# Linear attention and two expert layers on one core: attention steps of two batches moved by a slot, saved weight combinations paced anew, a result copy and six stores moved

## The chip, the cores and the metric

The kernel runs on one core of a Trainium2 chip. The metric is the device time of one execution in microseconds (us). An executed kernel has five engines with a queue of instructions each: PE (matrix products), DVE and ACT (elementwise work), POOL and SP (here mainly the issuing of DMAs). The engines work side by side and wait for each other by semaphores.

## The reference, cut to what matters

Four batches of eight heads, 576 positions and 64 channels per head. Attention is linear: a softmax over channels for q, one over positions for k, then two small products. Its result is x, 2304 tokens by 512, and passes through two layers:

```
q_s = softmax(q, over channels); k_s = softmax(k, over positions)
x = q_s @ (k_s^T @ v)                       # per batch and head
x = ((x @ w1) * (x @ w2)) @ w3 @ w_out      # 512 -> 1024 -> 512
p = domain_probs / sum(domain_probs)
out = sum over e of p[:, e] * (relu(x @ e1[e]) @ e2[e])   # four experts
```

All inputs are fp32, and every product here is made of three matmuls of a high and a low part (`mm3`, lines 106 to 110; `split`, line 101, makes the two parts: the high one by ACT, line 102, the low one by DVE, line 103).

## The kernel before, in words

The program has three stages. **Stage one** (0 to 272 us in the profile) reads the weights of the first layer, folds `w3 @ w_out` into one matrix `W`, and computes attention batch by batch. **Tokens** go in five chunks of 512, the last of 256 (numbers 0 to 4). For each chunk and each of eight slices `f` of the hidden layer, `ab_step` makes `x @ w1` and `x @ w2`, `h_step` splits their product into `h`, and `y_step` adds `h @ W` into four PSUM banks; `y_out(c)` copies the four banks into `yt` tiles (ACT, line 517) and stores them to DRAM. The `y_step`s of chunks 0 and 1 come in one loop of 16 steps, the Y loop (217 to 272 us), since `W` is ready only then. Chunk 2 follows (to 360 us), then chunks 3 and 4 together (to 455 us).

**Attention** of the later batches is cut into steps that stand in tables by slot and run between the steps of the layer: for each pair of heads `k_max` in slot s (its PE work is `mt`, lines 212 and 216, its ACT copy `mx`, line 220), `k_exp` in s+1, `k_v` in s+2 (PE `kv`, line 245, ACT `bd`, line 257), `x_stage` in s+3 (PE `xp`, line 326, then a split into `x`). The queries go in `q_exp`, `q_norm` and `q_turn` (PE `qt`, line 313). In batches 2 and 3 `mt`, `kv`, `qt` and `xp` share two PSUM banks.

**Combinations.** The third stage multiplies blocks of the experts' weights by a scheme with fewer products, and wants sums of weight blocks, split in two. For many expert blocks these are made ahead ("cooked") and saved to DRAM: `cooking` loads raw weights into two buffers (`e1r`, `e2r`, 1 MB), `cook` lists the parts and sums; a part is a `split` into one of five `eo` tiles (ACT, then DVE), a sum is one DVE instruction (line 586); `save_e` stores an `eo` by an SP DMA (line 606; `e_a<-eo`, `e_s<-eo`, `e_t<-eo`, `e_b<-eo`). `cook_some(k)` takes the next k of these. In the program before it takes two per step of the Y loop from its fourth step, four per step of chunk 2, and eight per step of chunks 3 and 4, and all that are left in step `NF-3`.

**Stage three** (455 to 1168 us) is the expert layer: PE lines 876 and 950, with loads of weights `eg`. At its end `store` (line 836) writes each of 18 tiles of 128 tokens in two halves by SP DMAs; the last six tiles come last.

The program's order is not the order on an engine: a scheduler that estimates times lays out the instructions of every engine, so moving a step in the code moves other rows too. The sections below show such rows. What fixes an order without a wait is `hold(key, inst)`, which makes an instruction stand behind those in `gate[key]`.

Of the kernel before, what the change touches and what calls it, by code (L numbers as in the profile page):

```python
# [8 lines left out]
F32 = mybir.dt.float32  # L9
# [4 lines left out]
ALU = mybir.AluOpType  # L14
# [23 lines left out]
X_SLOT = [AB0, AB1, REST, REST + 8]  # L38
# [16 lines left out]
def linear_attention_moe_kernel(ctx: ExitStack, tc, q, k, v, w1, w2, w3, wo, dp, e1, e2, out):  # L55
    nc = tc.nc
    w1, w2, w3, wo = (w.bitcast(I32) for w in (w1, w2, w3, wo))
    B, H, S, D = q.shape
    NT, DM = out.shape
    NF = w1.shape[1] // 256  # L60
    E = e1.shape[0]
    P = 128
# [6 lines left out]
    QP, QR = 64, 9  # L69
# [15 lines left out]
    def gran(name):  # L85
        return gp.tile([P, 2, 512], F32R, tag="g", name=name)

    def raw(name, pool=gp):
        return pool.tile([P, 1024], F32, tag="g", name=name)
# [10 lines left out]

    def split(hi, lo, src, eng=nc.vector):
        i = nc.scalar.activation(out=hi, in_=src, func=ACTF.Copy)  # L102
        eng.tensor_tensor(out=lo, in0=src, in1=hi.bitcast(F32), op=ALU.subtract)  # L103
        return i

    def mm3(ps, w_hi, w_lo, r_hi, r_lo, first, last, shared=False):
        kw = {"skip_group_check": True} if shared else {}
# [4 lines left out]
    gate = {}  # L112

    def after_inst(inst, other):
        tc.add_manual_dep(inst.ins, other.ins.name, ORDER, reason="order")

    def hold(key, inst):
        for other in gate.get(key, []):
            after_inst(inst, other)
# [231 lines left out]
    before, mid, after = {}, {}, {}  # L351

    def put(d, slot, f, *a):
        d.setdefault(slot, []).append((f, a))

    def run(d, slot):
        for f, a in d.pop(slot, []):
            f(*a)

    for b in range(B):  # L360
        for j in range(2):
            s = Q_SLOT[b][j]
            if b > 0:
                put(before, s - 2, load_q, b, j)
            put(before, s, q_exp, b, j)
            put(before, s + 1, q_norm, b, j)
            for g in range(3):
                put(after, s + 1, q_turn, b, j, g)
        for i, hp in enumerate(PAIRS):
            s = K_SLOT[b][i]  # L370
            if b > 0:
                put(before, s - 3, load_kv, b, hp)
            put(before, s, k_max, b, hp)
            put(before, s + 1, k_exp, b, hp)
            put(mid, s + 2, k_v, b, hp)
            put(after, min(s + 3, X_SLOT[b] - 1), x_stage, b, hp)

# [65 lines left out]
    def load_w12(c, f):  # L445
        for i in range(2):
            g = gran("wg")
            gate["dma"] = [nc.sync.dma_start(out=g.bitcast(F32), in_=w12d[f, i])]
            w12.setdefault((c, f), []).append(g)
        if c == NC - 2:  # L450
            w12[NC - 1, f] = w12[c, f]
# [8 lines left out]
    hg, yps, Wg, prods, ps_z = {}, {}, {}, {}, []  # L460
# [22 lines left out]
    def h_step(c, f):  # L483
        n = chunks[c][1]
        h = gran("h")
        split(h[:, 0, 0:n], h[:, 1, 0:n], prods[c, f // 2][:, f % 2, 0:n])
        if f % 2:
            del prods[c, f // 2]
        hg[c, f] = h
# [22 lines left out]
    def y_out(c):  # L512
        j0, n = chunks[c]
        for dd in range(2):
            t = raw("yt").rearrange("p (k f) -> p k f", k=2)
            for k in range(2):
                nc.scalar.activation(
                    out=t[:, k, 0:n], in_=yps[c, 2 * dd + k], func=ACTF.Copy
                )
            nc.sync.dma_start(out=yd[:, 2 * dd:2 * dd + 2, j0:j0 + n], in_=t[:, :, 0:n])  # L520
# [38 lines left out]
    ewd, ew, tok, yraw = {}, {}, {}, {}  # L559
# [11 lines left out]
    def load_e(kind, n, pool):  # L571
        e, m = n // 2, n % 2
        r = pool.tile([P, 2048], F32, tag="R", name=f"{kind}r")
        for hf in range(2):
            o = 512 * hf + 256 * m
            if kind == "e1":
                dst = r.rearrange("p (h k f) -> p h k f", h=2, k=KT)
                src = e1[e][:, o:o + 256].rearrange("(k p) f -> p k f", p=P)
            else:
                dst = r.rearrange("p (h u f) -> p h u f", h=2, u=2)  # L580
                src = e2[e][o:o + 256, :].rearrange("(u p) f -> p u f", p=P)
            nc.sync.dma_start(out=dst[:, hf], in_=src)
        return dst
# [4 lines left out]
    def cook(kind, n, r, part):  # L588
        q11, q12, q21, q22 = QUARTERS[kind](r)
        if kind == "e1":  # L590
            return [
                part("a11", q11), part("a12", q12), part("a22", q22),
                minus(q22, q21, q22, ALU.add), minus(q21, q11, q21), part("s1", q22),
                minus(q11, q22, q11), part("s3", q21), minus(q12, q12, q11),
                part("s2", q11), part("s4", q12),
            ]
        return [
            part("b11", q11), part("b21", q21), part("b22", q22),
            minus(q11, q12, q11), minus(q12, q22, q12), part("t1", q11),
            minus(q22, q22, q11), part("t3", q12), minus(q21, q21, q22),  # L600
            part("t2", q22), part("t4", q21),
        ]

    def save_e(kind, n, name, g):
        ewd[kind, n, name] = d = dr.tile([P, 2, 2, 256], F32, name=f"{kind}_{n}_{name}")
        nc.sync.dma_start(out=d, in_=g.bitcast(F32))
# [4 lines left out]
    def cooking(pool):  # L611
        raws_e, waiting = {}, []

        def ask(i):
            if i < len(COOKED):
                raws_e[i] = load_e(*COOKED[i], pool)

        def part_of(kind, n):
            def part(name, src):
                def do():  # L620
                    g = pool.tile([P, 2, 2, 256], F32R, tag="o", name="eo", bufs=NOUT)
                    split(g[:, 0], g[:, 1], src)
                    waiting.append((kind, n, name, g))
                return do
            return part

        ask(0)
        yield
        for i, (kind, n) in enumerate(COOKED):
            ask(i + 1)  # L630
            for do in cook(kind, n, raws_e.pop(i), part_of(kind, n)):
                do()
                while len(waiting) > 2:
                    save_e(*waiting.pop(0))
                yield
        while waiting:
            save_e(*waiting.pop(0))
# [32 lines left out]
    def slot(s, *steps):  # L670
        run(before, s)
        for f, *args in steps:
            f(*args)
            run(mid, s)
        run(mid, s)
        run(after, s)
# [69 lines left out]
    kitchen = ExitStack()  # L746
# [3 lines left out]
    def cook_some(k):  # L750
        for _ in range(k):
            next(cooks, None)

    for i, (c, f) in enumerate(steps):
        if c == 1 and f >= NF - 2:
            load_w12(2, f - NF + 2)
        if i + 4 < len(steps):
            h_step(*steps[i + 4])
        slot(Y0 + i, (y_step, c, f))
        if i > 2:  # L760
            cook_some(2)
        if f == NF - 1:
            y_out(c)

# [13 lines left out]
        run(after, REST + f)  # L778
    x_free(2)
    y_step(2, NF - 1)  # L780
    y_out(2)
    att.close()
    two = ExitStack()
    ps_z.append(two.enter_context(tc.tile_pool(name="ps_z", bufs=2, space=PSUM)))
    for f in range(NF):
        if f + 2 < NF:
            load_w12(3, f + 2)
        run(before, REST + NF + f)
        for c in (3, 4):
            ab_step(c, f)  # L790
            h_step(c, f)
            cook_some(4)
        run(mid, REST + NF + f)
        for c in (3, 4):
            if f > 0:
                y_step(c, f - 1)
        run(after, REST + NF + f)
        if f == NF - 3:
            cook_some(200)
            kitchen.close()  # L800
            yp_ = ctx.enter_context(tc.tile_pool(name="yp", bufs=1, side="right"))
            tp = ctx.enter_context(
                tc.tile_pool(name="tok", bufs=7, side="right", reuse_waits="tile")
            )
            ep = ctx.enter_context(
                tc.tile_pool(name="e", bufs=9, side="right", reuse_waits="tile")
            )
            load_y(0)
            first_tok = tset(0)
        if f >= NF - 3:  # L810
            for g in first_tok[4 * (f - NF + 3):4 * (f - NF + 4)]:
                g()
        if f == NF - 2:
            for name in USE["e1"]:
                load_cooked("e1", 0, name)
    for c in (3, 4):
# [12 lines left out]
    acc, blocks, hs = {}, {}, {}  # L829
    NN = 3 * NGE  # L830

    def store(t):
        for hf in range(2):
            b, n = divmod(2 * t + hf, QR)
            dst = out[S * b:S * b + S].rearrange("(q n) d -> n q d", n=QR)
            nc.sync.dma_start(out=dst[n], in_=acc[t][QP * hf:QP * hf + QP])

    def run_some(works, k, of):
        for work in works:
# [222 lines left out]
```

## Time and profile before

| what | us |
|---|---|
| median of three runs | 1174.22 (1173.98 to 1175.68) |
| the profiled execution | 1177.03 |
| its span, first to last instruction | 1175.3 |
| PE busy in it | 1132.6 |
| DVE, ACT, POOL busy | 866.1, 534.8, 49.4 |
| mean granted PE clock | 0.988 of full |

The span is what the rows below measure; the execution's own time is 1.7 us longer. A window row gives the busy time of each engine in a stretch, then the clock granted to PE as a share of its full 2.4 GHz (0.50 is 1.2 GHz), the busy share of the DMA engines and their GB/s. The chain is the work that ended last, followed back from the end. A timeline row gives a start, a duration, and in brackets how long the engine stood before it and what it waited for.

### The profile page before, as it was taken

To read this page: it belongs to the slowest core of one execution; us is meant where nothing else is said; L and a number is where in the kernel's file an instruction comes from. 1 tells how busy PE (TensorE), PEld (TensorE's weight loads), DVE (VectorE), ACT (ScalarE), POOL (GpSimd) and SP (SyncE) were. 2 spreads that over 40 slices of the span, in tenths; PEclk is the share of its full clock that TensorE was granted. 3 is DMA by queue.
4 is the path that set the end of the run, shared out by engine and by line. 5 is a ranking of instruction groups with operands and counts; after the bars stand their busy time and mean duration, and the time that the engine had idled before them with its cause. 6 is when DMAs were issued, how large, how long until landed. Compare 5 with 4: busy or idle time off the path is not lost.

```text
span 1175.3 us, 18720 instructions
## 1 busy us (share of the span) xinstructions
PE 1132.6 (96%) x7048; PEld 1053.3 (90%) x7048; DVE 866.1 (74%) x1428; ACT 534.8 (46%) x982; POOL 49.4 (4%) x70
## 2 busy tenths in 40 slices
PE   5889999989999999999999999999999999999997
PEld 4666888768788889999999999999999999999997
DVE  7898867765557312999989987777779777777776
ACT  4655535554445213655545543444445344444441
POOL 0002300012001000000000000000000000000000
PEclk9889999989999999999999999999999999999999
DMA  9998960699899903877786888777777787777773
GB/s 241 276 349 275 358 224 21 218 370 413 287 369 356 352 29 134 332 287 286 287 286 252 281 309 302 251 253 249 251 251 247 257 300 253 250 252 251 247 254 96
DMA packets 127418, 310.12 MB, mean 264 GB/s; under 512 B 31968, under 2 KB 52960, under 8 KB 127328
## 3 DMA queue, kind: packets, MB, share of 16 engines
q1 hardware_dynamic: 127328, 308.92, 76.6%
q8 instruction: 56, 0.92, 0.3%
q14 instruction: 34, 0.28, 0.1%
HBM read 232.33 MB, written 76.55 MB: 263 GB/s over the span
## 4 chain that ended last, share of the span: by engine, by line
PE 86%; DVE 4%; DMA 4%; ACT 1%; SPq 1%; issue 1%; DVEq 0%; ACTq 0%
PE hp L876 29%; PE op L950 27%; PE ab L108 6%; PE ab L109 6%; PE ab L110 6%; PE y L108 2%; PE y L109 2%; PE y L110 2%; PE kv L245 1%; DVE acc L934 1%; DMA qr<-in_q_dram 1%; DMA eg<-e_b 1%; PE W L108 1%; PE W L109 1%; PE W L110 1%
## 5 line engine op out<-in xcount | busy, mean ns | idle before, releaser
L950 PE MATMUL op<-eg,h 128*128 128x256 f32 x3024 | 379.9, 280 | 0.9 <-DMA eg<-e_b 0.8
L876 PE MATMUL hp<-t,eg 128*128 128x384 f32 x2016 | 376.8, 336 | 0.9 <-DVE acc L934 0.9
L950 PEld LDWEIGHTS op<-eg,h 128*128 128x128 f32 x3024 | 373.4, 188 | 1.4 <-PE hp L876 1.1
L876 PEld LDWEIGHTS hp<-t,eg 128*128 128x128 f32 x2016 | 344.6, 188 | 2.8 <-DVE acc L934 1.9
L934 DVE SCALAR_TENSOR_TENSOR acc<-op,prob,acc 128x256 f32<-128x256 f32 (+1 forms) x396 | 197.2, 527 | 43.2 <-PE op L950 43.1
L102 ACT ACTIVATE h<-blk 128x768 fp32r<-128x768 f32 x168 | 138.0, 842 | 144.1 <-DVE blk L586 109.9
L103 DVE TENSOR_TENSOR h<-blk,h 128x768 fp32r<-128x768 f32 x168 | 157.2, 951 | 24.0 <-ACT h L102 23.9
L859 ACT ACTIVATE blk<-hp 128x384 f32<-128x384 f32 x192 | 90.5, 489 | 140.9 <-PE hp L876 139.1
L863 DVE TENSOR_TENSOR blk<-hp,blk 128x384 f32<-128x384 f32 x144 | 79.4, 556 | 67.3 <-PE hp L876 66.8
L108 PE MATMUL ab<-x,wg 128*128 128x512 f32 (+1 forms) x320 | 122.4, 384 | 4.7 <-ACT wg L102 2.7
L109 PE MATMUL ab<-x,wg 128*128 128x512 f32 (+1 forms) x320 | 120.7, 377 | 0.2 <-ACT x L347 0.2
L110 PE MATMUL ab<-x,wg 128*128 128x512 f32 (+1 forms) x320 | 120.1, 378 | 0.0
L865 ACT ACTIVATE blk<-blk 128x768 f32<-128x768 f32 x72 | 60.6, 845 | 73.7 <-DVE blk L863 72.2
L586 DVE TENSOR_TENSOR blk<-blk 128x768 f32<-128x768 f32 x96 | 91.4, 952 | 0.5
L108 PEld LDWEIGHTS ab<-x,wg 128*128 128x128 f32 x320 | 61.2, 192 | 16.1 <-ACT wg L102 3.2
L109 PEld LDWEIGHTS ab<-x,wg 128*128 128x128 f32 x320 | 61.8, 193 | 10.9 <-ACT x L347 0.8
L480 DVE TENSOR_TENSOR ah<-ab,ah 128x512 f32<-128x512 f32 (+1 forms) x40 | 25.4, 634 | 62.3 <-PE ab L110 56.0
L110 PEld LDWEIGHTS ab<-x,wg 128*128 128x128 f32 x320 | 61.6, 193 | 10.6
L103 DVE TENSOR_TENSOR eo<-e2r,eo 128x512 fp32r<-128x512 f32 x56 | 39.8, 719 | 29.9 <-ACT eo L102 29.9
L109 PE MATMUL y<-h,W 128*128 128x512 f32 x128 | 50.9, 399 | 1.4 <-DVE h L103 1.4
L102 ACT ACTIVATE h<-ah 128x512 fp32r<-128x512 f32 (+1 forms) x40 | 22.8, 589 | 64.0 <-DVE ah L480 64.0
L110 PE MATMUL y<-h,W 128*128 128x512 f32 x128 | 50.2, 398 | 0.0
(98 smaller groups left out, 1068.2 us busy)
## 6 DMA issues: line engine op xcount, KB each, us to landing
eg<-e_t SPq DMA_DIRECT2D x96, 512.0 KB, 4.6
eg<-e_b SPq DMA_DIRECT2D x72, 512.0 KB, 5.2
eg<-e_s SPq DMA_DIRECT2D x68, 512.0 KB, 4.4
eg<-e_a SPq DMA_DIRECT2D x51, 512.0 KB, 4.6
wg<-w SPq DMA_DIRECT2D x48, 512.0 KB, 8.8
f<-in_moe_w_dram SPq DMA_DIRECT2D x32, 512.0 KB, 6.4
e_t<-eo SPq DMA_DIRECT2D x32, 512.0 KB, 6.2
e_s<-eg SPq DMA_DIRECT2D x28, 512.0 KB, 3.9
```

Source lines behind the costliest of these rows:

```text
L102: i = nc.scalar.activation(out=hi, in_=src, func=ACTF.Copy)
L103: eng.tensor_tensor(out=lo, in0=src, in1=hi.bitcast(F32), op=ALU.subtract)
L108: nc.tensor.matmul(out=ps, lhsT=w_hi, rhs=r_hi, start=first, stop=False, **kw)
L109: nc.tensor.matmul(out=ps, lhsT=w_hi, rhs=r_lo, start=False, stop=False, **kw)
L110: nc.tensor.matmul(out=ps, lhsT=w_lo, rhs=r_hi, start=False, stop=last, **kw)
L586: return lambda: nc.vector.tensor_tensor(out=dst, in0=x, in1=y, op=op)
L859: nc.scalar.activation(out=block(name)[:, u], in_=src, func=func)
L863: nc.vector.tensor_tensor(out=x[:, u], in0=src, in1=x[:, u], op=ALU.add)
L865: nc.scalar.activation(out=x, in_=x, func=ACTF.Relu)
L876: nc.tensor.matmul(out=q, lhsT=w[:, sw, kt, P * u:P * u + P], rhs=t[b][:, kt, st], start=new and kt == 0 and i == 0, stop=kt == 1 and i == ...
L934: nc.vector.scalar_tensor_tensor(out=dst, in0=src, scalar=prob[:, T, e:e + 1], in1=dst, op0=ALU.mult, op1=ALU.add,)
L950: nc.tensor.matmul(out=q[:, c:c + DH], lhsT=g[:, sh, u, P * i:P * i + P], rhs=w[:, sw, u], start=new and u == 0 and j == 0, stop=u == 1 an ...
```

## The change

Five parts. `x_stage` of batches 2 and 3 stands one slot later. The parts of the combinations stand behind the low half of `h` of chunk 0, slice 3 (an order, not a wait). The Y loop takes one combination step where it took two, and the rest is taken, and the kitchen closed, one step later in chunks 3 and 4 (`NF-2`), for which two pools are opened earlier. `y_out(2)` stands inside the first step of chunks 3 and 4, behind both chunks' `ab_step` and `h_step`, where it stood ahead of that loop. The second halves of the last six tiles are stored over ACT's DMA queue.

```
@@ -100,8 +100,8 @@
 
     def split(hi, lo, src, eng=nc.vector):
         i = nc.scalar.activation(out=hi, in_=src, func=ACTF.Copy)
-        eng.tensor_tensor(out=lo, in0=src, in1=hi.bitcast(F32), op=ALU.subtract)
-        return i
+        j = eng.tensor_tensor(out=lo, in0=src, in1=hi.bitcast(F32), op=ALU.subtract)
+        return i, j
 
     def mm3(ps, w_hi, w_lo, r_hi, r_lo, first, last, shared=False):
         kw = {"skip_group_check": True} if shared else {}
@@ -373,7 +373,7 @@
             put(before, s, k_max, b, hp)
             put(before, s + 1, k_exp, b, hp)
             put(mid, s + 2, k_v, b, hp)
-            put(after, min(s + 3, X_SLOT[b] - 1), x_stage, b, hp)
+            put(after, min(s + (4 if b > 1 else 3), X_SLOT[b] - 1), x_stage, b, hp)
 
 
 
@@ -483,7 +483,9 @@
     def h_step(c, f):
         n = chunks[c][1]
         h = gran("h")
-        split(h[:, 0, 0:n], h[:, 1, 0:n], prods[c, f // 2][:, f % 2, 0:n])
+        lo = split(h[:, 0, 0:n], h[:, 1, 0:n], prods[c, f // 2][:, f % 2, 0:n])[1]
+        if (c, f) == (0, 3):
+            gate["cook"] = [lo]
         if f % 2:
             del prods[c, f // 2]
         hg[c, f] = h
@@ -619,7 +621,8 @@
             def part(name, src):
                 def do():
                     g = pool.tile([P, 2, 2, 256], F32R, tag="o", name="eo", bufs=NOUT)
-                    split(g[:, 0], g[:, 1], src)
+                    for i in split(g[:, 0], g[:, 1], src):
+                        hold("cook", i)
                     waiting.append((kind, n, name, g))
                 return do
             return part
@@ -758,7 +761,7 @@
             h_step(*steps[i + 4])
         slot(Y0 + i, (y_step, c, f))
         if i > 2:
-            cook_some(2)
+            cook_some(1)
         if f == NF - 1:
             y_out(c)
 
@@ -778,9 +781,10 @@
         run(after, REST + f)
     x_free(2)
     y_step(2, NF - 1)
-    y_out(2)
     att.close()
     two = ExitStack()
+    yp_ = ctx.enter_context(tc.tile_pool(name="yp", bufs=1, side="right"))
+    tp = ctx.enter_context(tc.tile_pool(name="tok", bufs=7, side="right", reuse_waits="tile"))
     ps_z.append(two.enter_context(tc.tile_pool(name="ps_z", bufs=2, space=PSUM)))
     for f in range(NF):
         if f + 2 < NF:
@@ -790,27 +794,25 @@
             ab_step(c, f)
             h_step(c, f)
             cook_some(4)
+        if f == 0:
+            y_out(2)
         run(mid, REST + NF + f)
         for c in (3, 4):
             if f > 0:
                 y_step(c, f - 1)
         run(after, REST + NF + f)
         if f == NF - 3:
-            cook_some(200)
-            kitchen.close()
-            yp_ = ctx.enter_context(tc.tile_pool(name="yp", bufs=1, side="right"))
-            tp = ctx.enter_context(
-                tc.tile_pool(name="tok", bufs=7, side="right", reuse_waits="tile")
-            )
-            ep = ctx.enter_context(
-                tc.tile_pool(name="e", bufs=9, side="right", reuse_waits="tile")
-            )
             load_y(0)
             first_tok = tset(0)
         if f >= NF - 3:
             for g in first_tok[4 * (f - NF + 3):4 * (f - NF + 4)]:
                 g()
         if f == NF - 2:
+            cook_some(200)
+            kitchen.close()
+            ep = ctx.enter_context(
+                tc.tile_pool(name="e", bufs=9, side="right", reuse_waits="tile")
+            )
             for name in USE["e1"]:
                 load_cooked("e1", 0, name)
     for c in (3, 4):
@@ -833,7 +835,8 @@
         for hf in range(2):
             b, n = divmod(2 * t + hf, QR)
             dst = out[S * b:S * b + S].rearrange("(q n) d -> n q d", n=QR)
-            nc.sync.dma_start(out=dst[n], in_=acc[t][QP * hf:QP * hf + QP])
+            eng = nc.scalar if hf and t >= NT // P - 6 else nc.sync
+            eng.dma_start(out=dst[n], in_=acc[t][QP * hf:QP * hf + QP])
 
     def run_some(works, k, of):
         for work in works:
```

In the changed kernel a line of `y_out` is 519 and not 517; the lines up to 480 are the same.

Where the instructions moved, at three places. **PE at the last `y` of chunk 0** (about 238 us in the profile before). Numbers tell the buffers: `bd_2067` is made from `kv_2069`. Before:

```order
L216 MATMUL mt_2048<-ident_75,mt_2050 128x128
L245 MATMUL kv_2069<-vt_1807,ek_1990 128x130 x5
L326 MATMUL xp_2106<-qT_2007,bd_2067 128x288
L326 MATMUL xp_2108<-qT_2007,bd_2067 128x288
L245 MATMUL kv_2152<-vt_1894,ek_2089 128x130 x5
L108 MATMUL y0_2134<-h_1931,W_1527 128x512
L109 MATMUL y0_2134<-h_1931,W_1527 128x512
```

After (`bd_2049` is made from `kv_2051`, which now stands 72 rows ahead, inside the products of slice 6 of chunk 0):

```order
L108 MATMUL y3_1778<-h_1883,W_1739 128x512
L109 MATMUL y3_1778<-h_1883,W_1739 128x512
L110 MATMUL y3_1778<-h_1883,W_1739 128x512
L245 MATMUL kv_2124<-vt_1894,ek_2077 128x130 x5
L326 MATMUL xp_2135<-qT_2001,bd_2049 128x288
L108 MATMUL y0_2106<-h_1917,W_1527 128x512
L109 MATMUL y0_2106<-h_1917,W_1527 128x512
L110 MATMUL y0_2106<-h_1917,W_1527 128x512
```

`xp` followed the `kv` it depends on at once; now the `kv` ahead of it is the next pair's, which is read 42 rows later. **PE at the start of chunk 2** (about 274 us; `mt`, `qt` share two banks). Before, the two `qt` stand behind the first twelve products of chunk 2, of which the last four are shown:

```order
L110 MATMUL ab_2401<-x2_1_937,wg_2298 128x512
L108 MATMUL ab_2401<-x2_3_1000,wg_2298 128x512
L109 MATMUL ab_2401<-x2_3_1000,wg_2298 128x512
L110 MATMUL ab_2401<-x2_3_1000,wg_2298 128x512
L313 MATMUL qt_2545<-ident_75,qe_2383 128x128 x3
L313 MATMUL qt_2550<-ident_75,qe_2383 128x128 x3
```

After:

```order
L109 MATMUL y3_2109<-h_2198,W_1739 128x512
L110 MATMUL y3_2109<-h_2198,W_1739 128x512
L216 MATMUL mt_2345<-ident_75,mt_2347 128x128
L216 MATMUL mt_2415<-ident_75,mt_2417 128x128
L313 MATMUL qt_2490<-ident_75,qe_2335 128x128 x3
L313 MATMUL qt_2495<-ident_75,qe_2335 128x128 x3
L108 MATMUL ab_2353<-x2_0_781,wg_2256 128x512
```

The `qt` moved ahead of those products, right behind the two `mt` whose banks they need. **ACT at the end of chunk 2** (about 360 us). Before, the four `yt` copies stand ahead of the first copy of chunk 3 (`ah_3133`):

```order
L102 ACTIVATE eo_3518<-e2r_3256 128x512
L517 ACTIVATE yt_3110<-y0_2515 128x512
L517 ACTIVATE yt_3110<-y1_2516 128x512
L517 ACTIVATE yt_3114<-y2_2517 128x512
L517 ACTIVATE yt_3114<-y3_2518 128x512
L479 ACTIVATE ah_3133<-ab_3134 128x512
```

After (`ah_3123` is chunk 4's first slice, `ah_3079` chunk 3's second):

```order
L479 ACTIVATE ah_3123<-ab_3124 128x256
L102 ACTIVATE eo_3530<-e2r_3220 128x512
L102 ACTIVATE h_3152<-ah_3123 128x256
L519 ACTIVATE yt_3167<-y0_2467 128x512
L519 ACTIVATE yt_3167<-y1_2468 128x512
L519 ACTIVATE yt_3171<-y2_2469 128x512
L519 ACTIVATE yt_3171<-y3_2470 128x512
```

The copies of the first slices of chunks 3 and 4 come first now, then the four `yt` copies.

## Rows read from the trace of the kernel before

**Rows 1.** Page, parts 1 and 4: busy times, and the chain's shares.
```profile
PE 1132.6 (96%) x7048; PEld 1053.3 (90%) x7048; DVE 866.1 (74%) x1428; ACT 534.8 (46%) x982; POOL 49.4 (4%) x70
...
PE 86%; DVE 4%; DMA 4%; ACT 1%; SPq 1%; issue 1%; DVEq 0%; ACTq 0%
```

**Rows 2.** Windows: stretch, length, PE, PEld, DVE, ACT, POOL busy, clock, DMA share, GB/s.
```profile
40.00:45.00 5.00, 2.44 (x12) 1.53 (x10) 2.77 (x3) 2.10 (x7) 0.41 (x2) 0.98 1.03 207
45.00:50.00 5.00, 4.56 (x14) 3.78 (x15) 3.95 (x12) 3.12 (x8) 0.00 (x0) 0.50 0.97 281
85.00:90.00 5.00, 3.49 (x17) 1.95 (x15) 4.91 (x6) 3.95 (x10) 1.42 (x2) 1.00 1.04 348
90.00:95.00 5.00, 4.88 (x25) 4.09 (x26) 4.32 (x10) 3.96 (x11) 3.39 (x3) 1.00 1.07 268
...
240.00:245.00 5.00, 1.32 (x5) 1.01 (x5) 4.67 (x9) 3.50 (x9) 2.74 (x3) 0.78 1.06 392
245.00:250.00 5.00, 4.97 (x15) 3.44 (x15) 3.82 (x11) 3.98 (x10) 0.32 (x2) 0.50 1.01 305
...
320.00:325.00 5.00, 4.25 (x22) 3.17 (x21) 3.58 (x9) 4.12 (x11) 2.34 (x3) 1.00 0.95 310
```

**Rows 3.** Timeline of PE, four places where it stood or began.
```profile
220.77 0.50 PE L109 MATMUL y<-h,W 128*128 128x512 f32 x1 [1.41 <-DVE h L103]
...
238.98 1.48 PE L245 MATMUL kv<-vt,ek 128*128 128x130 f32 x10
...
274.58 0.89 PE L216 MATMUL mt<-ident,mt 128*128 128x128 f32 x4 [0.28 <-DVE mt L214]
...
361.89 0.39 PE L108 MATMUL ab<-x,wg 128*128 128x256 f32 x1 [1.29 <-ACT ah L479]
```

**Rows 4.** Chain from 225 to 262 us: start, duration, what.
```profile
229.90 7.12 DMA e_s<-eo
237.13 0.64 ACT eo L102
...
238.51 4.77 DMA e_t<-eo
243.38 0.29 ACT bd L257
...
244.13 2.26 PE xp L326 x4
246.42 2.83 PE kv L245 x10
...
250.83 0.43 PE y L108
...
254.45 0.23 PE y L110
...
258.11 0.97 PE xp L326 x4
```

**Rows 5.** Timeline of ACT: the `eo` backlog, then the copies at the chunks' ends.
```profile
226.09 0.67 ACT L102 ACTIVATE eo<-e2r 128x512 fp32r<-128x512 f32 x1
...
275.11 0.68 ACT L220 ACTIVATE mx<-mt 128x128 f32<-128x128 f32 x2
...
359.28 2.06 ACT L517 ACTIVATE yt<-y 128x512 f32<-128x512 f32 x4 [4.04 <-PE y L110]
```

**Rows 6.** Timeline at the end: DVE's last sums and SP's stores.
```profile
1164.98 7.54 SPq L836 DMA_DIRECT2D out_dram<-acc  x12
1167.05 1.14 DVE L934 SCALAR_TENSOR_TENSOR acc<-op,prob,acc 128x256 f32<-128x256 f32 x2 [0.39 <-PE op L950]
```

**Rows 7.** Line 836: issue ns min/median/max, first and last start; then landing.
```profile
L836 SPq DMA_DIRECT2D out_dram<-acc x36: 470/587/697, 706.3 to 1171.9; - x36
...
DMA to landing us min/median/max: 2.2/2.5/6.6
```

**Rows 8.** Timeline of SP: first loads of saved combinations for stage three.
```profile
394.49 1.50 SPq L667 DMA_DIRECT2D eg<-e_a  x2
```

More of the change, by code (lines that the diff above doesn't have):

```diff
@@ L102, in split @@
         i = nc.scalar.activation(out=hi, in_=src, func=ACTF.Copy)
-        eng.tensor_tensor(out=lo, in0=src, in1=hi.bitcast(F32), op=ALU.subtract)
-        return i
+        j = eng.tensor_tensor(out=lo, in0=src, in1=hi.bitcast(F32), op=ALU.subtract)
+        return i, j
     def mm3(ps, w_hi, w_lo, r_hi, r_lo, first, last, shared=False):
@@ L375, in linear_attention_moe_kernel @@
             put(mid, s + 2, k_v, b, hp)
-            put(after, min(s + 3, X_SLOT[b] - 1), x_stage, b, hp)
+            put(after, min(s + (4 if b > 1 else 3), X_SLOT[b] - 1), x_stage, b, hp)
     jobs = [(x, f) for f in range(NF) for x in ("a", "b")]
@@ L485, in h_step @@
         h = gran("h")
-        split(h[:, 0, 0:n], h[:, 1, 0:n], prods[c, f // 2][:, f % 2, 0:n])
+        lo = split(h[:, 0, 0:n], h[:, 1, 0:n], prods[c, f // 2][:, f % 2, 0:n])[1]
+        if (c, f) == (0, 3):
+            gate["cook"] = [lo]
         if f % 2:
@@ L621, in do @@
                     g = pool.tile([P, 2, 2, 256], F32R, tag="o", name="eo", bufs=NOUT)
-                    split(g[:, 0], g[:, 1], src)
+                    for i in split(g[:, 0], g[:, 1], src):
+                        hold("cook", i)
                     waiting.append((kind, n, name, g))
@@ L760, in linear_attention_moe_kernel @@
         if i > 2:
-            cook_some(2)
+            cook_some(1)
         if f == NF - 1:
@@ L780, in linear_attention_moe_kernel @@
     y_step(2, NF - 1)
-    y_out(2)
     att.close()
     two = ExitStack()
+    yp_ = ctx.enter_context(tc.tile_pool(name="yp", bufs=1, side="right"))
+    tp = ctx.enter_context(tc.tile_pool(name="tok", bufs=7, side="right", reuse_waits="tile"))
     ps_z.append(two.enter_context(tc.tile_pool(name="ps_z", bufs=2, space=PSUM)))
@@ L792, in linear_attention_moe_kernel @@
             cook_some(4)
+        if f == 0:
+            y_out(2)
         run(mid, REST + NF + f)
@@ L798, in linear_attention_moe_kernel @@
         if f == NF - 3:
[L799 to L807, printed above, removed]
             load_y(0)
@@ L813, in linear_attention_moe_kernel @@
         if f == NF - 2:
+            cook_some(200)
+            kitchen.close()
+            ep = ctx.enter_context(
+                tc.tile_pool(name="e", bufs=9, side="right", reuse_waits="tile")
+            )
             for name in USE["e1"]:
@@ L835, in store @@
             dst = out[S * b:S * b + S].rearrange("(q n) d -> n q d", n=QR)
-            nc.sync.dma_start(out=dst[n], in_=acc[t][QP * hf:QP * hf + QP])
+            eng = nc.scalar if hf and t >= NT // P - 6 else nc.sync
+            eng.dma_start(out=dst[n], in_=acc[t][QP * hf:QP * hf + QP])
     def run_some(works, k, of):
```

## The prediction

> **What bounds the kernel now.** I read the page first. PE is busy for 1132.6 of 1175.3 us and the chain that ended last runs over PE for 86% [rows 1]. So the change can win only where PE stands or runs slowly, and at the two ends. From the first product of stage three (455 us) to the end PE's order is the same in both kernels, so I looked at 0 to 455 us and at the tail.
>
> The windows of 5 us show where PE loses time [rows 2]: above all 240 to 245, where it is busy for 1.32 us of 5. The windows also show what such a stand does to the clock. After 2.56 us of idle PE in 40 to 45 and after 3.68 in 240 to 245 the granted clock of the next window is 0.50 (1.2 GHz); after 1.51 us in 85 to 90 it stays at 1.00. PE's timeline names the waits that the change can touch: 1.41 us at 220.77 for DVE's low half of `h`, the `kv` of 238.98 behind which the long stand comes, 0.28 at 274.58, and 1.29 at 361.89 for an ACT copy `ah` [rows 3].
>
> The chain from 225 to 262 us tells why PE stood at 240 [rows 4]. `xp` at 244.13 needs `bd`, ACT's copy of the `kv` issued just ahead of it. ACT made it only at 243.38, because it works in order and had `eo` parts before it; these wait for a free one of five tiles, that is for stores (7.12 us for `e_s<-eo`, then 4.77 for `e_t<-eo`). From the `eo` at 226.09 [rows 5] to that `bd` ACT was 17.3 us in this backlog. Then PE ran at half clock: the four `xp` took 2.26 us (0.97 at 258.11), ten `kv` 2.83 (1.48 at 238.98), a `y` product 0.43 (0.23 later) [rows 3, 4].
>
> **The change, part by part.**
>
> *A. The stand at 240.* From the `kv` at 238.98 to the end of the `xp` at 258.11 + 0.97 pass 20.1 us. At full clock and with no wait the same work takes 1.48 + 1.48 for twenty `kv`, 2 x 0.97 for eight `xp` and 30 `y` x 0.23 = 6.9, in sum 11.8 [rows 3, 4]. So 8.3 us are lost: 3.7 standing, 4.6 at half clock. With `x_stage` a slot later, the order of PE has `kv_2051` 72 rows ahead of the `xp` that needs it; 67 of these are `y` products, 67 x 0.23 = 15 us of cover. `kv_2124` is read 42 rows later, 41 of them `y`, 9.4 us in all. The backlog of ACT also begins later, as the parts stand behind `h`, and its order has 22 parts ahead of chunk 2 where it had 27. The first `bd` needs some 4 us of ACT even behind six parts of 0.67 [rows 5], and 15 cover that. A new need takes some of it back: `kv_2124` and the `xp` behind it use the PSUM bank of the `xp` before, which is free when ACT and DVE have split it, and ACT has seven parts ahead of that split. I put 0.8 us on this, about one part of 0.67 that ACT has just begun. **Gain 7.5**; bounds 0 (the backlog holds `bd` or that split as before) and 8.3.
>
> *B. The parts behind `h`.* The 1.41 us at 220.77 come from DVE doing sums and parts ahead of `h` [rows 3]. Now six `h` come first, on ACT and DVE. But PE's `y` then waits for ACT's copies of `W`, and the `mx` of a `kv` stands behind those `h`. I count about 0.8 us of waits left: **gain 0.6**, bounds 0 and 1.4.
>
> *C. The start of chunk 2.* The two `qt` stand right behind two `mt`, and need the banks that ACT's `mx` copies set free. Those stand behind the four `yt` copies and a part. In the trace `mx` ends at 275.11 + 0.68 = 275.8, 1.2 us behind the start of `mt` at 274.58 [rows 3, 5], and without the wait of 0.28 in front of it `mt` would start earlier. So PE stands about 1.5 us where it stood 0.28. Before, twelve products covered this. **Loss 1.2**; bounds 0 and, with one more part of 0.67 and its wait for a store, some 4. Behind the `qt` all of chunk 2 waits.
>
> *D. Inside chunk 2.* PE idles 0.75 us in 320 to 325 [rows 2], with ACT and DVE well loaded. In the new order the nearest `bd` there is 15 rows from its `xp` and the rest further. I take **gain 0.7**, bounds -1 and 0.75.
>
> *E. `y_out(2)` later.* The 1.29 us at 361.89 exist because four `yt` copies of 2.06 us stand ahead of `ah` [rows 3, 5]. Now both `ah` of the first slices come first, and 24 products of chunk 3's second slice stand ahead of the first `y` that needs the copied banks: 24 x 0.23 = 5.5 us for 2.06 us of copies. **Gain 1.3**, bounds 0 and 1.3. On SP the two `yt` stores move behind a load of raw weights; what reads them is a load for stage three, so no cost.
>
> *F. The rest at half pace.* Thirteen steps move to chunks 3 and 4 and end the combinations about two slices later, some 22 us. The first loads of them for stage three issue at 394.5 [rows 8] and would issue near 416. Their reader comes at 455, and the slowest kind of landing on the way was 7.12 [rows 4], so 30 us are left. **0**. If the cover were gone, each us late would be one of PE.
>
> *G. The tail.* SP issues the last twelve stores from 1164.98 for 7.54 us, at 0.59 each, the last at 1171.9, and the span ends 2.5 + 0.9 us behind [rows 6, 7]. The last sum is done at 1167.05 + 1.14 = 1168.2. With six on each queue, SP's and ACT's (ACT has nothing else by then) both wait for that sum at the fourth tile, and two more issues follow: last start about 1168.2 + 2 x 0.6 = 1169.4. **Gain 2.5**, bounds 0 (ACT's issues are dear, or share something) and 3.1 (one issue behind the last sum). No DMA of ACT exists in this trace, so its price is taken from SP's, the nearest row. The Trainium skill (DMA: Bandwidth & Descriptors, "Issuing engines are not separate DMA queues") says that two issuing engines share the same DMA engines and save only issue time, "usually small relative to the DMA itself"; by that word the gain would be near 0 and the sum 8.9. The rows say that here issue is the larger: 7.54 us against a landing of 2.5.
>
> **Sum.** 7.5 + 0.6 - 1.2 + 0.7 + 1.3 + 2.5 = 11.4 us. The profiled execution took 1177.0, which gives 1165.6 on its scale. It lies 2.8 above the median of 1174.2, and the forecast for the median is **1162.8**.
>
> **The rivals.**
>
> 1. *The clock falls at the start of chunk 2.* The new stand C of 1.5 us is like the 1.51 of 85 to 90 that kept the clock; at 2.56 it fell [rows 2]. One more part ahead of `mx` on ACT would bring it there: 1.0 us more of standing, and 4.6 of half clock as in A. 1162.8 + 5.6 = **1168.4**. For it: ACT's order has parts between the `yt` copies. Against: the parts' tiles are mostly free there. The Trainium skill (TensorE: Matmul & The Clock Gate, "HAM oscillation") warns of just this, that a wait between stretches of products starts the next one at half clock. Rows 2 agree for the long waits and not for the short.
>
> 2. *The backlog stays.* Half pace removes only five of 27 parts, and the stores share full DMA engines (share 1.06 in 240 to 245 [rows 2]). So the change hardly does what it says, ACT's split or `bd` still comes late, and A is worth nothing: 1162.8 + 7.5 = **1170.3**.
>
> 3. *The stores gain nothing*, since both queues feed the same engines: 1162.8 + 2.5 = **1165.3**.
>
> 4. *Slower: the last x of batch 2 is late.* `xp_2184` is now followed by 41 `y` (9.4 us), four `mt`, two `qt` and nine products until chunk 2 reads it, 12 us in all; before there were 66 `y`, 15 us, ahead of chunk 2 alone. Its split waits in ACT's backlog. The trace's backlog of 17.3 us would make PE stand 5 us, with half clock behind it 10, nearly the whole gain. From 19 us it decides against the change; at 24 (that backlog and one more store of 7.12) PE stands 12 us and loses 4.6: 1162.8 + 16.6 = **1179.4**. For it: all of chunk 2 waits on that split. Against: the backlog starts later, is thinner, and DVE and ACT have gaps in 255 to 270.
>
> **How the numbers follow.** Chances: the forecast 0.55, the clock 0.12, the backlog 0.15, the stores 0.10, the late x 0.08. The lower end of the range takes every bound on the good side (8.3 + 1.4 + 0 + 0.75 + 1.3 + 3.1 = 14.9, so 1159.3) and a little for the spread of the runs: 1158.5. The upper end takes in rivals 1 to 3 with 1.2 for C or D at a worse value: 1171.5. A measurement of this kernel can tell about 0.2% (2.35 us) from no change. Faster by more than that means below 1171.9: the forecast, the clock, the stores and half of the backlog's case, 0.55 + 0.12 + 0.10 + 0.07 = 0.84. Within it: the rest of that case, 0.08. Slower: 0.08.
>
> **What would show it.** Right: no window near 235 to 260 with PE below 4 of 5 us and none at 0.50 there (A); a wait of 1 to 2 us at the first `qt` of chunk 2, clock kept (C); no wait for `ah` near 350 (E); last stores starting about 1.2 us behind DVE's last sum, on both queues (G). Wrong: a stand for `bd` or for an x split above 2 us with half clock behind it, PE waiting for `eg` at the start of stage three (F), or ACT's stores starting later than SP's.

## The result, and the profile after

The changed kernel takes 1162.18 us (median of 4 runs, 1159.55 to 1162.37); the kernel before took 1174.1 beside it (4 runs). The ratio is 0.989, with a 95% interval of 0.987 to 0.991: faster by 12 us, clear of 0.2%. The forecast was 1162.8, in a range of 1158.5 to 1171.5. The profiled execution took 1162.17, with a span of 1160.4. Of its page, part 1, one line of part 3 (DMA queues; the tenth is ACT's) and part 4:

```profile
PE 1127.0 (97%) x7048; PEld 1050.2 (91%) x7048; DVE 868.4 (75%) x1428; ACT 534.7 (46%) x982; POOL 46.8 (4%) x70
...
q10 hardware_dynamic: 480, 0.79, 0.2%
...
PE 86%; DVE 6%; DMA 5%; SPq 2%; issue 1%; ACT 1%; DVEq 0%; ACTq 0%
```

PE still bounds it [rows 1]. The windows of the changed kernel where [rows 2] showed loss, and the one new place (columns as there):

```profile
215.00:235.00 20.00, 19.98 (x90) 15.55 (x90) 17.24 (x29) 15.06 (x31) 2.35 (x3) 1.00 0.75 255
235.00:260.00 25.00, 25.00 (x114) 20.48 (x113) 16.55 (x32) 14.05 (x31) 0.73 (x4) 1.00 1.04 390
...
260.00:265.00 5.00, 4.00 (x21) 3.16 (x19) 2.94 (x9) 2.86 (x8) 0.00 (x0) 1.00 1.02 417
320.00:325.00 5.00, 5.00 (x23) 4.12 (x22) 3.75 (x8) 2.35 (x6) 0.20 (x1) 1.00 1.01 367
...
350.00:355.00 5.00, 5.00 (x32) 4.43 (x31) 1.50 (x4) 3.41 (x8) 2.19 (x8) 1.00 0.84 315
```

From 215 to 260 us PE never stands and the clock stays full, though in 235 to 260 the DMA engines are as full as before (share 1.04, 1.05 before). PE's timeline there has `xp` and `kv` in their new places, at full speed, and one wait:

```profile
234.03 1.13 PE L326 MATMUL xp<-qT,bd 128*128 128x288 f32 x4
237.77 1.47 PE L245 MATMUL kv<-vt,ek 128*128 128x130 f32 x10
239.17 0.75 PE L326 MATMUL xp<-qT,bd 128*128 128x288 f32 x2
...
265.07 0.88 PE L313 MATMUL qt<-ident,qe 128*128 128x128 f32 x6 [1.07 <-ACT mx L220]
```

That 1.07 us is the only wait that the profile names for PE between 205 and 460 us. The timeline at the tail, which answers to [rows 6]:

```profile
1151.94 4.34 SPq L839 DMA_DIRECT2D out_dram<-acc  x6
1151.94 5.27 ACTq L839 DMA_DIRECT2D out_dram<-acc  x6
1154.00 1.14 DVE L937 SCALAR_TENSOR_TENSOR acc<-op,prob,acc 128x256 f32<-128x256 f32 x2 [0.39 <-PE op L953]
```

**A measure steadier than the total.** Up to the start of chunk 1 the order of PE is the same in both kernels, yet that start lay anywhere from 118.97 to 122.28 us in the profiles of this study: behind the long waits of the first 110 us PE runs at half clock for a longer or a shorter time (in 45 to 50 us the granted clock was 0.50 in the profile before and 0.66 in that after). So I measure from the first product of chunk 1 to the first product of stage three (`hp`). These are the two rows in the kernel before (455.10 - 121.79 = 333.31):

```profile
121.79 0.47 PE L108 MATMUL ab<-x,wg 128*128 128x512 f32 x1
...
455.10 0.51 PE L876 MATMUL hp<-t,eg 128*128 128x384 f32 x2
```

and in the changed kernel (442.03 - 120.00 = 322.03):

```profile
120.00 0.48 PE L108 MATMUL ab<-x,wg 128*128 128x512 f32 x1
...
442.03 0.68 PE L879 MATMUL hp<-t,eg 128*128 128x384 f32 x3
```

Other kernels with PE's and ACT's order of before gave 333.34 and 333.49, others with the order after 322.02 twice. The change is worth 11.3 us in this stretch and 1.8 behind DVE's last sum (7.1 to the end of the span before, 5.2 after). The other 1.8 us of the two profiles' 14.9 are the start, 121.79 against 120.00, which the change did not touch. From the first `hp` to DVE's last sum both took 713.1 us.

### The profile page after: what moved, and what is told of

Its sections match the earlier page's. It is cut to its first block, busy times and chain, and to the rows that moved or that the text cites. A ratio compares the mean times of both kernels' runs of the same rounds, so it can differ in the third digit from the quotient of the medians.

```text
span 1160.4 us, 18707 instructions
## 1 busy us (share of the span) xinstructions
PE 1127.0 (97%) x7048; PEld 1050.2 (91%) x7048; DVE 868.4 (75%) x1428; ACT 534.7 (46%) x982; POOL 46.8 (4%) x70
## 4 chain that ended last, share of the span: by engine, by line
PE 86%; DVE 6%; DMA 5%; SPq 2%; issue 1%; ACT 1%; DVEq 0%; ACTq 0%
PE hp L879 28%; PE op L953 26%; PE ab L110 5%; PE ab L108 5%; PE ab L109 5%; PE y L108 3%; PE y L110 2%; PE y L109 2%; DMA kr<-in_k_dram 2%; DVE acc L937 2%; PE kv L245 2%; PE W L108 1%; PE W L109 1%; PE W L110 1%; DVE h L103 1%; DVE blk L588 1%
## 5 line engine op out<-in xcount | busy, mean ns | idle before, releaser
L868 ACT ACTIVATE blk<-blk 128x768 f32<-128x768 f32 x72 | 60.6, 845 | 73.6 <-DVE blk L866 72.0
L109 PEld LDWEIGHTS ab<-x,wg 128*128 128x128 f32 x320 | 61.0, 191 | 10.8 <-ACT x L347 0.8
L110 PEld LDWEIGHTS ab<-x,wg 128*128 128x128 f32 x320 | 61.0, 191 | 10.8 <-DVE wg L103 0.5
L109 PE MATMUL y<-h,W 128*128 128x512 f32 x128 | 50.3, 395 | 0.0
L110 PE MATMUL y<-h,W 128*128 128x512 f32 x128 | 49.4, 392 | 0.0
L108 PE MATMUL y<-h,W 128*128 128x512 f32 x128 | 47.9, 404 | 0.0
```

The lines of the kernel that those rows point to most:

```text
L108: nc.tensor.matmul(out=ps, lhsT=w_hi, rhs=r_hi, start=first, stop=False, **kw)
L109: nc.tensor.matmul(out=ps, lhsT=w_hi, rhs=r_lo, start=False, stop=False, **kw)
L110: nc.tensor.matmul(out=ps, lhsT=w_lo, rhs=r_hi, start=False, stop=last, **kw)
L868: nc.scalar.activation(out=x, in_=x, func=ACTF.Relu)
```

## The experiments

Two theories. **S**, the prediction's: what counts is the distance in PE's order between a `kv` and the `xp` that reads its `bd`. **B**, the rival: what counts is how many parts ACT has to work off, thinned by the half pace and the order behind `h`. Each kernel's stretch from chunk 1 to stage three (one profiled execution), and its median with the ratio to the kernel before on the same chip. The kernels ran on several chips, so compare the ratios and not the medians:

| kernel | stretch, us | us | ratio (95%) |
|---|---|---|---|
| before | 333.31 | 1174.1 | 1 |
| changed | 322.04 | 1162.18 | 0.989 (0.987 to 0.991) |
| x_only | 324.69 | 1166.53 | 0.994 (0.992 to 0.996) |
| half_only | 333.49 | 1174.42 | 1.000 (0.999 to 1.001) |
| gate_only | 326.26 | 1168.12 | 0.993 (0.991 to 0.995) |
| no_x | 327.74 | 1167.25 | 0.993 (0.991 to 0.996) |
| no_gate | 324.12 | 1165.36 | 0.993 (0.990 to 0.995) |
| no_half | 322.02 | 1162.25 | 0.990 (0.987 to 0.992) |
| no_yout | 324.01 | 1165.17 | 0.992 (0.989 to 0.994) |
| x_five | 329.56 | 1168.83 | 0.993 (0.991 to 0.995) |
| qt_late | 321.98 | 1164.69 | 0.992 (0.989 to 0.994) |
| tail_only | 333.34 | 1173.5 | 0.999 (0.997 to 1.000) |
| tail_sorted | 322.02 | 1161.42 | 0.987 (0.985 to 0.989) |
| best | 321.97 | 1162.57 | 0.988 (0.986 to 0.989) |

**x_only**: the later `x_stage` alone.

```diff
-            put(after, min(s + 3, X_SLOT[b] - 1), x_stage, b, hp)
+            put(after, min(s + (4 if b > 1 else 3), X_SLOT[b] - 1), x_stage, b, hp)
```

> The kernel before with the later x_stage alone (batches 2 and 3). Theory S (the distance in PE's order between a kv and the xp that reads its bd sets the stand at 240): kv_2058 stands 51 rows ahead of the first xp of its pair's successor and over 70 ahead of its own, so the stand and the half clock behind it go, 8 us of the 8.3; no qt wait at chunk 2, since qt stays late here. About 1166 (1164.5 to 1168). Theory B (ACT's backlog of parts sets it, and half pace or the gate on the parts thinned it): all parts run as before, so ACT is as late as before, 1172 to 1175 with a stand above 2 us near 240.

1166.53, as S had it. In 235 to 260 PE is busy for all 25.00 us at full clock, with all parts at the old pace. The 8.6 us of its stretch are not the stand alone: PE waits 2.2 us for `W` and `h` between 217 and 224, where it waited 1.4 for `h`, and the wait for `ah` near 352 is 0.2 where it was 1.29, with `y_out(2)` at its old place.

**half_only**: one combination step per step of the Y loop.

```diff
         if i > 2:
-            cook_some(2)
+            cook_some(1)
```

> The kernel before with one combination step per step of the Y loop where it took two, alone. PE's order at 240 is that of before (kv, then at once the xp that needs it). Theory S: the stand stays, perhaps shorter, with half clock behind it: 1170 to 1174.5. Theory B: the thinner backlog frees ACT in time, the stand goes: 1164 to 1168.

No gain. PE's timeline has the stand of before, 3.68 us long, and `xp` and `kv` as slow as in [rows 4]:

```profile
242.05 2.26 PE L326 MATMUL xp<-qT,bd 128*128 128x288 f32 x4 [3.68 <-ACT bd L257]
244.34 2.83 PE L245 MATMUL kv<-vt,ek 128*128 128x130 f32 x10
```

**no_half**: the same line back in the changed kernel.

> The changed kernel with two combination steps per step of the Y loop, as before the change. PE's order up to chunk 2 is that of the changed kernel. Theory S (pace does nothing at 240): no wait for bd or x there, times as the changed kernel, 1161 to 1163.5. Theory B (the pace thins ACT's backlog, and the later x only goes with it): a stand above 1 us between 230 and 262, 1164 to 1168.

Equal to the changed kernel in the stretch (322.02). The pace of the code is worth nothing in either kernel. But these two runs do not test a thinner backlog, since the engines' order did not take up the new pace: in half_only PE's 7048 and ACT's 982 instructions stand in the order of before, and in no_half in that of the changed kernel. Up to chunk 2, ACT has the same 27 parts in the kernel before and in half_only (from `e2r` and `e1r`: count, duration in ns, first and last start in us; before, then half_only):

```profile
L102 ACT ACTIVATE eo<-e2r x20: 613/630/669, 226.1 to 274.1; 128x512 fp32r<-128x512 f32 x20
L102 ACT ACTIVATE eo<-e1r x7: 620/637/668, 213.4 to 225.6; 128x512 fp32r<-128x512 f32 x7
...
L102 ACT ACTIVATE eo<-e2r x20: 612/632/664, 223.9 to 272.0; 128x512 fp32r<-128x512 f32 x20
L102 ACT ACTIVATE eo<-e1r x7: 620/633/671, 211.2 to 223.4; 128x512 fp32r<-128x512 f32 x7
```

What tells S from B is how late `bd` came. In the kernel before the `kv` ended at 238.98 + 1.48 [rows 3] and ACT's two `bd` at 243.38 + 0.61, 3.5 us behind it. In the changed kernel, PE's first `kv` of the Y loop and ACT's `bd`s:

```profile
219.64 1.58 PE L245 MATMUL kv<-vt,ek 128*128 128x130 f32 x10
...
224.94 0.64 ACT L257 ACTIVATE bd<-kv,rs 64x64 f32<-64x64 f32 x2
...
241.16 0.64 ACT L257 ACTIVATE bd<-kv,rs 64x64 f32<-64x64 f32 x2
```

They ended 4.4 us behind this `kv` and 2.6 behind that of 237.77. Behind the first `kv` of the Y loop it was 3.1 us in x_only, 4.2 in gate_only and no_x, 5.3 in no_gate. So `bd` came about as late where PE did not stand as where it stood; what differs is the work between `kv` and `xp`. That is S, and B, by which ACT would be free in time, falls.

**gate_only**: the order behind `h` alone, in the kernel before (its main lines; `gate` is set as in the change).

```diff
-                    split(g[:, 0], g[:, 1], src)
+                    for i in split(g[:, 0], g[:, 1], src):
+                        hold("cook", i)
```

> The kernel before with the order alone that puts the parts behind h of chunk 0, slice 3. In PE's order this moves the kv of the stand from 1 row to 13 rows ahead of the xp that reads it (twelve y, 2.8 us). Theory S (distance in PE's order): the stand shrinks from 3.7 by about 2.8, to near 1.4 as in the run of the changed kernel with x at its old slot, half clock partly behind it; the 1.4 for h near 220 go; from the start of chunk 1 to DVE's last sum 4 to 5.5 us less than before, total 1168.5 to 1171. Rival (the gate only shifts the parts, ACT's backlog just comes later): stand above 3 us, 1172.5 to 1175.

1168.12, a little below the bounds of S. The stretch fell by 7.05, of which 1.4 is the wait for `h`; from chunk 1 to DVE's last sum 7.3 us are gained where I expected 4 to 5.5, as I had counted with some half clock. The stand is 1.4 us for `bd`, and 0.5 more at the next `kv`, as S says for 13 rows of distance. It is not a store that makes `bd` late here: ACT stood 3.05 us for POOL's `kr`, and DVE's `rs`, which `bd` also needs, stood behind a part and a sum that came late by it. The windows (columns as in [rows 2]) keep the full clock:

```profile
235.00:240.00 5.00, 3.63 (x15) 2.66 (x16) 2.18 (x5) 1.97 (x5) 1.56 (x3) 1.00 0.97 317
240.00:245.00 5.00, 4.49 (x23) 3.34 (x23) 2.27 (x7) 4.38 (x11) 0.32 (x2) 1.00 1.06 402
245.00:250.00 5.00, 5.00 (x24) 4.13 (x23) 4.93 (x9) 2.80 (x7) 0.00 (x0) 1.00 1.09 377
```

**no_x**: the changed kernel with `x_stage` back at s + 3.

> The changed kernel with x_stage back at its old slot. In PE's order the kv stands 13 rows ahead of the xp that reads it, twelve y products, 2.8 us. Theory S: PE stands for bd again near 240, 1 to 3 us, and if the stand is long the clock falls: 1165 to 1170. Theory B: the pace and the gate hold ACT free, no stand, 1162 to 1163.

1167.25, as S had it, with runs from 1162.71 to 1169.29; the profiled one is the longest. The waits are again 1.4 us for `bd` and 0.5 behind it, but in its windows the clock fell:

```profile
240.00:245.00 5.00, 3.45 (x13) 2.69 (x14) 2.40 (x7) 3.72 (x10) 0.20 (x1) 0.76 1.10 378
245.00:250.00 5.00, 5.00 (x14) 3.83 (x15) 4.30 (x9) 4.14 (x9) 0.12 (x1) 0.55 1.02 398
```

**no_gate**: the changed kernel without that order.

> The changed kernel without the order that puts the parts behind h of chunk 0, slice 3. In the order of PE qt moves away from the start of chunk 2. Theory S: no stand at 240 (kv far ahead of its xp); the 1.4 us for h near 220 come back, the 1.1 us for mx at chunk 2 go: 1162 to 1163.5. Theory B: with the gate gone the backlog is back, a stand above 2 us near 240 with half clock: 1167 to 1171.

No stand at 240, so S holds there, but the total, 1165.36, is 2 us above what I expected. PE waits 1.6 us for ACT's copy of `W` near 217 and 0.3 for `h`: in this order three parts stand on ACT ahead of the `W` copies. The wait at `qt` is gone, and the stretch is 2.1 longer than the changed kernel's.

**no_yout**: the changed kernel with `y_out(2)` back at the end of chunk 2.

```diff
     y_step(2, NF - 1)
+    y_out(2)
     att.close()
...
-        if f == 0:
-            y_out(2)
```

> The changed kernel with y_out(2) back at the end of chunk 2. Theory S (the prediction's E): the four yt copies stand ahead of chunk 3's first ah again, PE waits 1.3 us for it near 350, all else as in the changed kernel: 1163 to 1164.5. Rival (the later x alone moved enough of ACT's work: with it and y_out at its old place the wait for ah was 0.2): the wait is at most 0.3, 1161.5 to 1163.

1165.17, and the stretch grows by 2.0. The wait is back, and longer. PE's waits from 340 to 360 us (us in total, times, longest):

```profile
PE ab L108 <- ACT ah L479: 1.8, 1, 1.8
```

**x_five**: the changed kernel with `x_stage` yet a slot later.

```diff
-            put(after, min(s + (4 if b > 1 else 3), X_SLOT[b] - 1), x_stage, b, hp)
+            put(after, min(s + (5 if b > 1 else 3), X_SLOT[b] - 1), x_stage, b, hp)
```

> The changed kernel with x_stage of batches 2 and 3 yet one slot later (s+5). Theory S (distance needed is covered already): no wait for bd in either, so nothing more to gain at 240; in this order mt and qt stand behind the first products of chunk 2 again, so the 1.1 us there go: from the start of chunk 1 to DVE's last sum 0 to 1 less than the changed kernel's 1035.1, total 1161 to 1163. Rival (the prediction's late x): the last x of batch 2, now 40 rows ahead of chunk 2, comes late there or another wait takes its place: PE stands 1 us or more for an x near 262, 1163 to 1167.

1168.83. Both missed: 7.5 us of the gain are lost, and not at chunk 2. In its order `xp` x2 stand right ahead of `kv_2124`, which needs their PSUM banks:

```
L110 MATMUL y3_1778<-h_1883,W_1739 128x512
L326 MATMUL xp_2083<-qT_1824,bd_1949 128x288
L326 MATMUL xp_2085<-qT_1824,bd_1949 128x288
L245 MATMUL kv_2124<-vt_1894,ek_2066 128x130 x5
L108 MATMUL y0_2106<-h_1917,W_1527 128x512
```

The chain there (start, duration, what) is the one of [rows 4] with another last link: a part on ACT waits for a store, the split of `x` stands behind it, and `kv` waits for the split.

```profile
235.54 7.21 DMA e_s<-eo
242.86 0.64 ACT eo L102
...
244.13 0.46 DVE x L103
244.63 2.83 PE kv L245 x10
```

PE stood 4.73 us, then ran at half clock (0.61 in 245 to 250). In the changed kernel 13 rows, twelve of them `y`, lie between `xp` and that `kv`.

**tail_only**: the second halves of the last six tiles over ACT's queue, alone.

```diff
-            nc.sync.dma_start(out=dst[n], in_=acc[t][QP * hf:QP * hf + QP])
+            eng = nc.scalar if hf and t >= NT // P - 6 else nc.sync
+            eng.dma_start(out=dst[n], in_=acc[t][QP * hf:QP * hf + QP])
```

> The kernel before with the second halves of the last six tiles stored over ACT's queue, alone. Up to the last sum nothing changes. As the changed kernel's profile has it, the end comes 5.2 to 5.4 us behind DVE's last sum where it came 7.1 behind it: 1.8 us gained, about 1172.5. As the prediction had it (ACT issues like SP): 2.5, about 1172. If the two queues share what limits them: 0 to 0.5.

1173.5. The span ends 5.3 us behind DVE's last sum where it ended 7.1 behind it: 1.7 gained. The total's interval agrees and by itself can't tell it from nothing.

**tail_sorted**: in the changed kernel ACT's third store waits for a tile that DVE ends after the fourth. Here that tile's store is called later.

```diff
-                    if final:
+                    if final and i != 1:
                         store(6 * pr + 3 + i)
...
                         store(6 * pr + i)
+                        if i == 0:
+                            store(6 * pr + 4)
```

> The changed kernel with one of the last six tiles' stores called later, so that ACT's queue stores the tiles in the order in which DVE ends them (there the third waited for a tile that was done after the fourth). The last ACT store starts 0.8 us behind DVE's last sum where it was 1.5, and the span ends 4.6 to 4.8 us behind it where it was 5.3: 0.6 gained, too little for the total to tell (1161.5 to 1162.5). Rival (the landings of the two queues share a limit, as their 2.3 to 3.5 us against 2.4 hint): the end stays above 5.1.

The last ACT store starts 0.9 us behind the last sum, as meant, and the end comes 4.9 behind it (5.0 in best, with the same order): 0.2 to 0.4 gained of 0.6. The rest went into landings.

**qt_late**: `qt` of batch 3 held behind the first twelve products of chunk 2 (its main lines; `mm3` returns its last product for it).

```diff
+            if (c, f, i) == (2, 0, 0):
+                gate["qt"] = [m]
...
-            nc.tensor.transpose(ps[:, P * i:P * i + P], t[:, 3 * g + i], ident)
+            m = nc.tensor.transpose(ps[:, P * i:P * i + P], t[:, 3 * g + i], ident)
+            if b == 3:
+                hold("qt", m)
```

> The changed kernel with qt of batch 3 held, by an order, behind the first twelve products of chunk 2, where it stood before the change. Theory S: the wait of 1.1 us of qt for ACT's mx goes, nothing else moves: profile 1.0 us shorter from chunk 2 on, about 1161. Rival: the wait comes back one place later (another bank or the third qt), no gain: 1162.

The rival was right that nothing is gained, though its 1.0 us did not come back as one wait: the wait of 1.1 is gone, two new waits of 0.2 for `ah` are named, and the stretch is 0.06 shorter. PE's idle time in it fell from 1.09 to 0.45, so its busy time grew by 0.6; why stays open. The median, 1164.69, lies above both expectations; its five runs go from 1161.92 to 1168.03, and the profiled one is the shortest.

**best**: both repairs together.

> The changed kernel with both small repairs: qt of batch 3 held behind the first twelve products of chunk 2, and the stores in the order in which the tiles end. By the profiles 0.1 less from the start of chunk 1 to DVE's last sum, 0.6 less at the tail: 1160.5 to 1162. If the repairs are only moved into other waits: 1162 to 1164.

1162.57: no better than the changed kernel. tail_sorted has the lowest ratio of all, but its interval overlaps the changed kernel's, so only the profiles' 0.2 to 0.4 us at the tail speak for it.

## Why the prediction was right, step by step

*The forecast and its chief reason held.* The stand at 240 and the half clock behind it are gone. The single parts show the mechanism: more distance between `kv` and `xp` brings the gain (x_only 8.6 us of the stretch, gate_only 7.05), while `bd` comes as late as ever (4.4 us behind its `kv` in the changed kernel, 3.5 before). For *A* I had 7.5, keeping back 0.8 for the shared banks; that wait did not come, and PE stands nowhere from 235 to 260. But two statements beside it were wrong. I listed the 22 parts in place of 27 as a help and put the five down to half pace: the pace leaves all 27 (half_only), and where the later `x_stage` or the order behind `h` leaves 23 or 22, `bd` was not sooner by more than 0.4 us (x_only). And I gave the distance to `x_stage` alone: the order behind `h` also moves the `kv` up, by 12 rows, so either part alone brings most of the gain. For the order alone that hangs on the clock, which no_x lost behind the same stand.

*B* was too small: 1.4 in place of 0.6, as none of the 0.8 us of small waits that I counted came. no_gate shows what the order behind `h` is worth once `x` is later: 2.1 us of the stretch, with three parts ahead of the `W` copies as the price of leaving it out.

*C* was right in place and sign: 1.07 us for `mx` where I had 1.5, and the clock stayed at 1.00, so rival 1 did not happen. But as a term of the sum it was mis-sized: taking the wait away (qt_late) gained 0.06 us, not 1.1.

*D* was right: the 0.75 us of 320 to 325 are gone. *E* was right in kind and a little small: 1.3 forecast, 2.0 by no_yout, because without the move the wait in the new order would be 1.8 and not 1.29. What the move is worth hangs on the order around it: in x_only, without it, the wait was 0.2. *F* was right that it costs nothing, and the 22 us are luck. The first loads for stage three issue at 403.5, 38.5 us ahead of the first `hp` where it was 60.6 [rows 8], and nobody waits; but only 10.8 of these 22 us are a later issue, counted from the start of chunk 1, and the rest is stage three's earlier start. Nor does the half pace delay them: they issue 283.5 us behind that start in the changed kernel and in no_half, 283.1 in x_only, which has the old pace and the old place of the rest.

*G* was too large, 2.5 against 1.8. I took ACT's issues at SP's price and the landings as they were. ACT's six took 5.27 us, 0.50 to 0.85 each, its last store began 1.5 us behind the last sum and not 1.2, because of the tile order, and the landings grew to 3.5 us (2.4 before). Rival 3 did not happen. The Trainium skill's word that a second issuing engine saves only issue time (DMA: Bandwidth & Descriptors, "Issuing engines are not separate DMA queues") fits: the last store began 1.5 us behind the last sum where it had been 3.7, so what was saved is issue time, and it was not small here.

*The sum.* A to E came to 8.9 and the stretch shows 11.3; G brings 0.7 less. The 11.4 that I took off the profiled execution were then 13.1; the total moved by 12, with an interval of 10.8 to 14.8. So that the number came within 0.6 us is in part luck: A to E were 2.4 too small, G 0.7 too large, and the medians moved 1.2 less than the two profiles in the parts that changed. Rival 2 was right that half pace removes little (it removes nothing) and that `bd` still comes late, and wrong that A is then worth nothing: the lateness is covered. Rival 4 (the last x late at chunk 2) did not happen; x_five shows that its kin, an x split that is late for the banks, was the real danger, one slot away.

## What to carry to other kernels

Where an in-order engine has a backlog that waits for stores, look for its other clients: a step whose result the next matmul reads at once is the one that pays, and rows of other work put between producer and reader cover the lateness without removing it. Whether a thinner backlog would do as much is not shown here. Count that distance for both ends of the step, the value that it waits for and the PSUM bank that it holds, since moving it away from one moves it toward the other. Before you read a run, look whether its edit reached the order of the engines at all: half_only and no_half changed the code and neither PE's order nor ACT's. And where the total swings by some us for reasons ahead of the change, measure between two instructions of the profile instead: here the same order gave the same stretch within 0.2 us.

## What the runs showed of the hardware

The same stand, 1.4 us, four `xp` and 0.5 us, kept PE's clock at 1.00 in gate_only and sent it to 0.55 in no_x, with the same order of work on PE around it. The ten `kv` behind it (first gate_only, then no_x):

```profile
241.48 1.58 PE L245 MATMUL kv<-vt,ek 128*128 128x130 f32 x10 [0.51 <-DVE x L103]
...
242.76 2.83 PE L245 MATMUL kv<-vt,ek 128*128 128x130 f32 x10 [0.51 <-DVE x L103]
```

From the `kv` ahead of the stand to the `xp` of the next pair pass 16.9 us in the one (233.94 to 250.85) and 20.0 in the other (235.21 to 255.20). So a stand of some 2 us can cost its own length or 3.1 us more; which of the two, nothing in these profiles tells beforehand.

In the first 110 us the stands themselves differ, with the same instructions in the same order. In 40 to 45 us PE was idle for 2.56 us in the profile before, 2.15 in that of the changed kernel and 1.67 in x_only, and in 45 to 50 the granted clock was 0.50, 0.66 and 1.00. The windows of the changed kernel:

```profile
40.00:45.00 5.00, 2.85 (x13) 1.82 (x12) 2.31 (x3) 2.44 (x8) 0.41 (x2) 1.00 1.06 209
45.00:50.00 5.00, 4.09 (x14) 3.42 (x15) 4.26 (x11) 2.66 (x7) 0.00 (x0) 0.66 0.97 285
```

With stores on two queues at once, one 64 x 512 store lands in 2.3 to 3.5 us where it took 2.2 to 2.4 alone at the tail, and ACT's own issue is less even than SP's (line 839 of the changed kernel from 1150 us on, columns as in [rows 7]):

```profile
L839 SPq DMA_DIRECT2D out_dram<-acc x6: 466/550/588, 1151.9 to 1155.7; - x6
L839 ACTq DMA_DIRECT2D out_dram<-acc x6: 498/582/854, 1151.9 to 1156.7; - x6
...
DMA to landing us min/median/max: 2.3/2.7/3.5
```
